# A sign step moved to GpSimd and a subtraction moved to VectorE while the first MLP's weights are unpacked from float64

## The chip, the core and the metric

The kernel runs on one core of one Trainium2 chip. The metric is the device time of one execution in microseconds (us); the time of a kernel is the median of its runs. One execution is also recorded by the hardware profiler, and its rows are what this text reads. TensorE (PE) multiplies matrices, VectorE (DVE), ScalarE (ACT) and GpSimd (POOL) work elementwise on tiles of 128 partitions, and SyncE (SP) issues most transfers. Each engine takes its instructions strictly in the order in which the program put them; engines wait for one another through semaphores.

## What is computed

A delta-rule attention over 4 batches, 8 heads, 768 steps and 48 dimensions gives 3072 rows of 384. Two MLPs follow: one with 2048 hidden units and a PReLU, one with 1536 hidden units and a gated SiLU. Cut to what matters here:

```python
h = x @ w_in                       # 3072x384 by 384x2048
g = np.maximum(h, 0.0) + alpha * np.minimum(h, 0.0)
x = (g @ w_out).astype(np.float32) # 3072x2048 by 2048x384
g = x @ w_gate
val = x @ w_val
out = (silu(g) * val) @ w_out2
```

All weights reach the device as float64. The core has no float64 arithmetic in this kernel: it rebuilds each float32 from the two 32-bit words of a float64 with integer shifts.

## The kernel before

The sequence is cut into 24 chunks of 32 steps. For a window of four chunks the kernel transposes k and q, forms the products k k^T (tile `GL`), inverts a triangular system for all 32 lanes at once (`lanes`: VectorE takes ten columns of it, GpSimd the others, in alternating multiply and subtract steps named `tmp`/`X` and `tmg`/`X`), and then updates the state chunk by chunk (`do_KS`, `do_QS`, `do_U`, `do_S`, `do_Y`, `do_XT`). The result of two chunks is one block of 256 columns for the first MLP. A step of that MLP is `H1` (9 matmuls, then ScalarE and VectorE make the PReLU tile `pn`), `H1_parts` (ScalarE rounds it to the high part, GpSimd subtracts to get the low part, tile `gh`) and, two steps later, `O1` (9 matmuls). Matmul operands are split into a rounded high half and a low half, and three products are added.

The weights of the first MLP are 16 pairs (one slice of `w_in` and one of `w_out`, 384 elements each per partition). `all_w1` (L869) turns a pair from float64 into the two halves. For pair p:

- ScalarE scales the high words in place (`Cut.act`, L592).
- VectorE does three steps in `Cut.dve`: the sign bit into the one scratch tile `we` (z = 0, L597), the high word shifted and joined with that sign (z = 1, L599), the low word shifted and joined (z = 2, L603). Each works on 768 elements per partition.
- ScalarE copies the result, rounded, into the high half of the weight tile (L887).
- The low half is float32 minus high half (`lo`, L875): two operations of 384 elements, both on GpSimd.

The weight tile of pair p lies in the buffer that held the float64 words of pair p-1 (pool `ws`, 17 buffers), so the copy of pair p waits until the low half of pair p-1 has been made. `all_w1` is a generator. `prelude` takes 16 of its 49 steps by hand (`go(conv, ...)`); a list of due times (`at(...)`) spreads the rest over the first eleven MLP steps, three to a step, and so fixes where each instruction stands on its engine. A second user of `Cut`, the weights of the second MLP, works on 384 elements at a time, from due time 24 on.

```python
CONVS = C_A, C_B, C_C, C_D = (1, 3, 3, 1)
for i in range(CONV_N):
    at(-0.5 + i * CONV_END / CONV_N, go, conv)
```

In the names of instructions, `w_110` to `w_125` are the buffers of the float64 words of pairs 0 to 15.

Of the kernel before, what the change touches and what calls it, by code (L numbers as in the profile page):

```python
# [14 lines left out]
ALU = mybir.AluOpType  # L15
# [9 lines left out]
def kernel(  # L25
# [25 lines left out]
    nc = tc.nc  # L51
# [16 lines left out]
    W1_DVE = 16  # L68
# [508 lines left out]
    we = wstg.tile([128, 768], I32, name="we")  # L577
    wf_t = [we[:, 384:768].bitcast(F32), wstg.tile([128, 384], F32, name="wf")]

    class Cut:  # L580
# [13 lines left out]
        def dve(self, z):  # L594
            t, f = self.hi.bitcast(I32), self.f.bitcast(I32)
            if z == 0:
                nc.vector.tensor_scalar(we[:, 0 : self.n], t, -0x80000000, None, op0=ALU.bitwise_and)  # L597
            elif z == 1:
                nc.vector.scalar_tensor_tensor(  # L599
                    out=t, in0=t, scalar=3, in1=we[:, 0 : self.n], op0=ALU.logical_shift_left, op1=ALU.bitwise_or  # L600
                )
            else:
                nc.vector.scalar_tensor_tensor(  # L603
                    out=f, in0=self.lo, scalar=29, in1=t, op0=ALU.logical_shift_right, op1=ALU.bitwise_or
                )
# [18 lines left out]
    def load_w1(*slices, eng=nc.sync):  # L624
        for i in slices:
            load_wide(*w1_src(i), w1_64[i // 2][:, i % 2], eng)
# [242 lines left out]
    def all_w1():  # L869

        cuts = []

        def lo(p, z0, z1, eng):
            f = cuts[p].f.rearrange("p (a n) -> p a n", a=2)
            eng.tensor_tensor(w1[p][:, z0:z1, 1], f[:, z0:z1], w1[p][:, z0:z1, 0], ALU.subtract)  # L875

        for p in range(J1 + 1):
            while len(cuts) < min(J1, p + (1 if p == 0 else 2)):
                cuts.append(Cut(w1_64[len(cuts)]))
                cuts[-1].act()  # L880
            for z in range(3):
                if p < J1:
                    cuts[p].dve(z)
                if z == 0 and p > 0:
                    w1.append(ws.tile([128, 2, 2, 384], F32R, name="w", tag="w"))
                    f = cuts[p - 1].f.rearrange("p (a n) -> p a n", a=2)
                    nc.scalar.activation(out=w1[p - 1][:, :, 0], in_=f, func=AF.Copy)  # L887
                    lo(p - 1, 0, 1, nc.gpsimd)
                    if p <= W1_DVE:
                        lo(p - 1, 1, 2, nc.gpsimd)  # L890
                if z > 0 and W1_SP <= p + W1_AHEAD < J1:
                    load_w1(2 * (p + W1_AHEAD) + z - 1, eng=nc.scalar)
                if z == 1 and p > W1_DVE:
                    lo(p - 1, 1, 2, nc.vector)
                if p < J1 or z == 1:
                    yield

    conv = all_w1()

    def go(g, n=1):  # L900
# [251 lines left out]
```

## Time and profile before

| | us |
|---|---|
| runs | 1094.44, 1092.07, 1091.46 |
| median | 1092.07 |
| the profiled execution | 1094.43 |
| its span, first to last instruction | 1092.5 |
| TensorE busy | 1055.2 (97%) |
| VectorE busy | 603.6 (55%) |
| ScalarE busy | 389.9 (36%) |
| GpSimd busy | 359.5 (33%) |

The profiled execution is 2.36 us longer than the median of the runs. Busy shares are means over stages that differ: the unpacking of the 16 pairs lies between 10 and 116 us of the span, where GpSimd and VectorE are far busier than on average. A busy time holds whatever an engine spends inside an instruction, also when the instruction is held up by another engine. [...]

### The profile page before, as it was taken

How to read it: one execution, taken by the hardware profiler on the slowest of the kernel's cores; microseconds unless marked ns; L12 is line 12 of the kernel's file. 1: busy time of each engine (PE TensorE's matmuls, PEld its weight loads, DVE VectorE, ACT ScalarE, POOL GpSimd, SP SyncE). 2: the span in 40 equal slices, each digit the busy share in tenths (PEclk: the TensorE clock that was granted, in tenths of full speed). 3: DMA queues.
4: the chain of work that ended last, by engine and by line, in shares of the span. 5: the costliest groups of instructions: out<-in, count | busy, mean ns of one | idle time of the engine just before them, and what ended most of it. 6: DMA issues, size and time to landing. Idle time of an engine off the chain costs nothing.

```text
span 1092.5 us, 35673 instructions
## 1 busy us (share of the span) xinstructions
PE 1055.2 (97%) x15649; PEld 969.6 (89%) x15649; DVE 603.6 (55%) x1204; ACT 389.9 (36%) x841; POOL 359.5 (33%) x531
## 2 busy tenths in 40 slices
PE   6689899999999999999999999999999999999998
PEld 5588788999999999999999998888888888888887
DVE  5778865975895697489453453433333333333332
ACT  3556343343434334433444653222222222222211
POOL 3478852832563383366333541101001001010000
PEclk9669999999999999999999999999999999999999
DMA  9663042353344236330441541010010010100001
GB/s 196 184 192 105 10 103 53 62 122 95 70 69 134 66 62 139 90 82 11 118 130 56 159 135 54 1 58 1 1 58 1 18 42 1 58 1 1 29 1 29
DMA packets 165979, 76.34 MB, mean 70 GB/s; under 512 B 129824, under 2 KB 160576, under 8 KB 165824
## 3 DMA queue, kind: packets, MB, share of 16 engines
q1 hardware_dynamic: 160256, 66.28, 24.5%
q10 hardware_dynamic: 5184, 7.37, 2.2%
q8 instruction: 122, 2.00, 0.8%
q0 software_dynamic: 384, 0.41, 0.2%
q14 instruction: 33, 0.27, 0.1%
HBM read 57.52 MB, written 16.52 MB: 68 GB/s over the span
## 4 chain that ended last, share of the span: by engine, by line
PE 89%; POOL 4%; issue 2%; DVE 2%; DMA 1%; ACT 1%; SPq 0%; ACTq 0%; POOLq 0%; DVEq 0%
PE gv L772 27%; PE o L713 18%; PE h L682 18%; PE o L802 14%; PE pst L527 2%; PE pg L207 2%; PE pu L506 2%; PE py L548 2%; PE pk L462 2%; PE py L462 1%; POOL w L875 1%; DMA nat<-in_k_dram 1%; POOL gh L702 1%; POOL X L331 1%; POOL tmg L323 1%
## 5 line engine op out<-in xcount | busy, mean ns | idle before, releaser
L772 PE MATMUL gv<-x2s,w 128*128 128x512 f32 x1296 | 307.6, 391 | 0.0
L772 PEld LDWEIGHTS gv<-x2s,w 128*128 128x128 f32 x1296 | 242.5, 188 | 47.8
L713 PE MATMUL o<-gh,w 128*128 128x256 f32 x1728 | 246.2, 288 | 3.9 <-POOL gh L702 3.9
L682 PE MATMUL h<-xh,w 128*128 128x256 f32 x1152 | 241.2, 286 | 3.0 <-DVE pn L693 1.6
L702 POOL TENSOR_TENSOR gh<-pn,gh 128x256 fp32r<-128x256 f32 x192 | 155.3, 809 | 248.5 <-ACT gh L701 217.3
L713 PEld LDWEIGHTS o<-gh,w 128*128 128x128 f32 x1728 | 217.3, 189 | 11.5 <-POOL gh L702 5.1
L682 PEld LDWEIGHTS h<-xh,w 128*128 128x128 f32 x1152 | 192.2, 191 | 5.8 <-DVE pn L693 2.6
L693 DVE SCALAR_TENSOR_TENSOR pn<-pn,slope,h 128x256 f32<-128x256 f32 x192 | 91.3, 476 | 135.9 <-ACT pn L692 135.9
L682 PE MATMUL h<-xl,w 128*128 128x256 f32 x576 | 163.2, 283 | 0.1
L802 PE MATMUL o<-w,us 128*128 128x384 f32 x864 | 162.5, 337 | 0.0
L802 PEld LDWEIGHTS o<-w,us 128*128 128x128 f32 x864 | 151.9, 188 | 7.1 <-DVE os L815 1.4
L692 ACT ACTIVATE pn<-h,slope 128x256 f32<-128x256 f32 x192 | 90.4, 471 | 137.7 <-PE h L682 134.5
L784 DVE TENSOR_TENSOR sg<-sg,gv 128x512 f32<-128x512 f32 x72 | 49.5, 687 | 151.8 <-ACT sg L782 151.7
L701 ACT ACTIVATE gh<-pn 128x256 fp32r<-128x256 f32 x192 | 80.0, 417 | 145.0 <-DVE pn L693 143.2
L682 PEld LDWEIGHTS h<-xl,w 128*128 128x128 f32 x576 | 109.8, 191 | 0.6 <-DVE xl L574 0.6
L757 POOL TENSOR_TENSOR x2s<-x2r,x2s 128x512 fp32r<-128x512 f32 x15 | 19.3, 1320 | 266.6 <-ACT x2s L755 266.6
L789 ACT ACTIVATE us<-u 128x512 fp32r<-128x512 f32 x72 | 45.5, 632 | 171.2 <-DVE u L785 171.2
L782 ACT ACTIVATE sg<-gv 128x512 f32<-128x512 f32 x72 | 43.0, 597 | 159.3 <-PE gv L772 159.3
L790 DVE TENSOR_TENSOR us<-u,us 128x512 fp32r<-128x512 f32 x72 | 49.9, 693 | 54.8 <-ACT us L789 54.8
L785 DVE TENSOR_TENSOR u<-sg,gv 128x512 f32<-128x512 f32 x72 | 49.5, 688 | 49.3 <-PE gv L772 48.8
L331 DVE TENSOR_TENSOR X<-X,tmp 128x31 f32<-128x31 f32 (+29 forms) x155 | 65.0, 419 | 4.8
L323 DVE TENSOR_TENSOR tmp<-L,X 128x31 f32<-128x31 f32 (+29 forms) x155 | 59.5, 384 | 1.8
(120 smaller groups left out, 975.9 us busy)
## 6 DMA issues: line engine op xcount, KB each, us to landing
w<-in_moe_w_out_dram SPq DMA_DIRECT2D x19, 384.0 KB
wf<-w2d SPq DMA_DIRECT2D x36, 192.0 KB
k<-in_k_dram SPq DMA_DIRECT2D x96, 48.0 KB
x2d<-xs SPq DMA_DIRECT2D x12, 384.0 KB
w<-in_moe_w_gate_dram SPq DMA_DIRECT2D x12, 384.0 KB
w<-in_moe_w_val_dram SPq DMA_DIRECT2D x12, 384.0 KB
x2r<-x2d SPq DMA_DIRECT2D x24, 192.0 KB
v<-in_v_dram SPq DMA_DIRECT2D x88, 48.0 KB
```

The source lines that it names most:

```text
L323: eng.tensor_tensor(w, t.L[:, i + 1:C, i:i + 1].to_broadcast([128, n, m]), t.X[:, i:i + 1, c0:c0 + m].to_broadcast([128, n, m]), ALU.mult,)
L331: eng.tensor_tensor(Xv, Xv, w, ALU.subtract)
L682: nc.tensor.matmul(ps[:, 0:N1], w[:, a, kk * 128:kk * 128 + 128], x[b][:, kk, :], start=(i == 0), stop=(i == 3 * NK - 1),)
L692: nc.scalar.activation(out=g, in_=hv, func=AF.Relu, scale=slope[:, 0, j:j + 1])
L693: nc.vector.scalar_tensor_tensor(out=g, in0=g, scalar=slope[:, 1, j:j + 1], in1=hv, op0=ALU.mult, op1=ALU.add)
L701: nc.scalar.activation(out=gh[:, 0], in_=g, func=AF.Copy)
L702: nc.gpsimd.tensor_tensor(gh[:, 1], g, gh[:, 0], ALU.subtract)
L713: nc.tensor.matmul(o[:, dm // 2, (dm % 2) * N1:(dm % 2) * N1 + N1], w[:, a, dm * 128:dm * 128 + 128], g[:, b], start=(j == 0 and i == 0 an ...
L772: nc.tensor.matmul(p[:, 0:N2], w2[j, z][:, a, kk * 128:kk * 128 + 128], x[:, b, kk], start=(i == 0), stop=(i == 3 * NK - 1),)
L784: nc.vector.tensor_tensor(sg, sg, ps[0], ALU.mult)
L790: nc.vector.tensor_tensor(us[:, 1], u, us[:, 0], ALU.subtract)
L802: nc.tensor.matmul(o2_t[n][t][:, 0:DM], us[:, a, t * 128:t * 128 + 128], w[:, b, :], start=(j == 0 and i == 0), stop=(j == J2 - 1 and i == 2),
```

## The change

For the 768-element pairs, step z = 0 is issued on GpSimd: `is_lt 0.0` gives 1 or 0, the product with -2147483648.0 is written as an int32, which is the sign bit alone. The two low-half subtractions of 384 elements on GpSimd become one of 768 elements on VectorE, and it is issued one generator step later, between z = 1 and z = 2 of the next pair. The 384-element cuts of the second MLP keep the sign on VectorE.

```diff
         def dve(self, z):
             t, f = self.hi.bitcast(I32), self.f.bitcast(I32)
             if z == 0:
-                nc.vector.tensor_scalar(we[:, 0 : self.n], t, -0x80000000, None, op0=ALU.bitwise_and)
+                if self.n > 384:
+                    nc.gpsimd.tensor_scalar(
+                        we[:, 0 : self.n], self.hi, 0.0, -2147483648.0, op0=ALU.is_lt, op1=ALU.mult
+                    )
+                else:
+                    nc.vector.tensor_scalar(we[:, 0 : self.n], t, -0x80000000, None, op0=ALU.bitwise_and)
...
                     nc.scalar.activation(out=w1[p - 1][:, :, 0], in_=f, func=AF.Copy)
-                    lo(p - 1, 0, 1, nc.gpsimd)
-                    if p <= W1_DVE:
-                        lo(p - 1, 1, 2, nc.gpsimd)
                 if z > 0 and W1_SP <= p + W1_AHEAD < J1:
                     load_w1(2 * (p + W1_AHEAD) + z - 1, eng=nc.scalar)
-                if z == 1 and p > W1_DVE:
-                    lo(p - 1, 1, 2, nc.vector)
+                if z == 1 and p > 0:
+                    lo(p - 1, 0, 2, nc.vector)
```

VectorE, around the second pair (`w_111`), at 35 to 40 us of the trace: `TT` is the inverse that the first `do_U` multiplies with, `pi` a product it is corrected by. Before:

```order
L273 STREAM_TRANSPOSE TT<-X 128x16x32
L597 TENSOR_SCALAR we<-w_111 128x768
L599 SCALAR_TENSOR_TENSOR w_111<-w_111,we 128x768
L603 SCALAR_TENSOR_TENSOR w_111<-w_111 128x768
L439 TENSOR_TENSOR TT<-TT,pi 128x16x16
L597 TENSOR_SCALAR we<-w_112 128x768
```

And now:

```order
L273 STREAM_TRANSPOSE TT<-X 128x16x32
L604 SCALAR_TENSOR_TENSOR w_111<-w_111,we 128x768
L880 TENSOR_TENSOR w<-w_110,w 128x2x384
L608 SCALAR_TENSOR_TENSOR w_111<-w_111 128x768
L439 TENSOR_TENSOR TT<-TT,pi 128x16x16
L604 SCALAR_TENSOR_TENSOR w_112<-w_112,we 128x768
```

The sign has left VectorE's row and the subtraction of the pair before stands ahead of the correction of `TT`.

GpSimd, from its last transfers of v to the first unpacked pairs; `X` and `Dm` are cleared, `v` and `mt` are scaled. Before:

```order
L123 DMA v<-in_v_dram 32x8x48 x8
L263 MEMSET X 128x1024
L398 MEMSET Dm 128x32x16
L452 TENSOR_TENSOR v<-v,nn 128x384 x2
L195 TENSOR_TENSOR mt<-mt,mask 128x256 x2
L875 TENSOR_TENSOR w<-w_110,w 128x384 x2
L875 TENSOR_TENSOR w<-w_111,w 128x384 x2
```

And now:

```order
L123 DMA v<-in_v_dram 32x8x48 x8
L598 TENSOR_SCALAR we<-w_110 128x768
L263 MEMSET X 128x1024
L398 MEMSET Dm 128x32x16
L452 TENSOR_TENSOR v<-v,nn 128x384 x2
L195 TENSOR_TENSOR mt<-mt,mask 128x256 x2
L598 TENSOR_SCALAR we<-w_111 128x768
```

One sign stands for two subtractions of a pair, and the first sign comes ahead of the clearing of `X`.

VectorE at the end of the unpacking, at 106 to 116 us, where the second inversion begins with two transposes of `GL` into `L`. Before:

```order
L603 SCALAR_TENSOR_TENSOR w_124<-w_124 128x768
L693 SCALAR_TENSOR_TENSOR pn<-pn,slope,h_1990 128x256
L597 TENSOR_SCALAR we<-w_125 128x768
L599 SCALAR_TENSOR_TENSOR w_125<-w_125,we 128x768
L603 SCALAR_TENSOR_TENSOR w_125<-w_125 128x768
L693 SCALAR_TENSOR_TENSOR pn<-pn,slope,h_2057 128x256
L269 STREAM_TRANSPOSE L<-GL 128x512
```

And now:

```order
L608 SCALAR_TENSOR_TENSOR w_124<-w_124 128x768
L698 SCALAR_TENSOR_TENSOR pn<-pn,slope,h_1976 128x256
L604 SCALAR_TENSOR_TENSOR w_125<-w_125,we 128x768
L880 TENSOR_TENSOR w<-w_124,w 128x2x384
L608 SCALAR_TENSOR_TENSOR w_125<-w_125 128x768
L698 SCALAR_TENSOR_TENSOR pn<-pn,slope,h_2042 128x256
L880 TENSOR_TENSOR w<-w_125,w 128x2x384
L269 STREAM_TRANSPOSE L<-GL 128x512
```

Two subtractions came in, and the last of them stands right ahead of the first transpose.

## Rows read from the trace of the kernel before

**Rows 1.** The page: busy us (share of the span) and instructions of each engine.

```profile
PE 1055.2 (97%) x15649; PEld 969.6 (89%) x15649; DVE 603.6 (55%) x1204; ACT 389.9 (36%) x841; POOL 359.5 (33%) x531
```

**Rows 2.** Stages: length, busy us (instructions) of PE, PEld, DVE, ACT, POOL; clock, DMA.

```profile
34.00:56.00 22.00, 12.02 (x519) 10.38 (x519) 15.60 (x22) 11.90 (x20) 10.09 (x9) 0.59 0.63 158
56.00:84.00 28.00, 25.88 (x725) 24.00 (x725) 21.41 (x26) 15.29 (x30) 19.65 (x16) 0.71 0.66 185
84.00:116.00 32.00, 29.90 (x904) 27.10 (x904) 25.84 (x31) 18.51 (x39) 27.91 (x26) 1.00 0.32 84
116.00:148.00 32.00, 26.47 (x203) 24.21 (x202) 30.09 (x78) 11.21 (x31) 26.19 (x58) 1.00 0.30 57
...
200.00:640.00 440.00, 440.00 (x9148) 424.19 (x9146) 300.02 (x676) 191.47 (x448) 213.89 (x345) 1.00 0.38 92
```

**Rows 3.** Groups: busy us, mean ns, idle before; L875: min/median/max ns instead.

```profile
L875 POOL TENSOR_TENSOR w<-w,w x32: 1009/1225/1793, 36.6 to 113.6; 128x384 fp32r<-128x384 f32 x32
...
L597 DVE TENSOR_SCALAR we<-w 128x768 int32<-128x768 int32 x16 | 11.5, 717 | 3.7 <-ACT w L592 3.7
...
L599 DVE SCALAR_TENSOR_TENSOR w<-w,we 128x768 int32<-128x768 int32 x16 | 18.4, 1153 | 0.5
...
L603 DVE SCALAR_TENSOR_TENSOR w<-w 128x768 int32<-128x768 int32 x16 | 21.4, 1339 | 0.4
...
L693 DVE SCALAR_TENSOR_TENSOR pn<-pn,slope,h 128x256 f32<-128x256 f32 x192 | 91.3, 476 | 135.9 <-ACT pn L692 135.9
...
masks.py:199 POOL TENSOR_SCALAR_AFFINE_SELECT ident<-ident 128x128 f32<-128x128 f32 x1 | 0.3, 293 | 0.1
...
L263 POOL MEMSET X<- 128x1024 f32 x6 | 6.1, 1012 | 1.3 <-DVE L L269 1.3
```

**Rows 4.** Timeline, 35 to 40 us, VectorE and TensorE: start us, us, instruction [idle before].

```profile
35.01 0.56 DVE L597 TENSOR_SCALAR we<-w 128x768 int32<-128x768 int32 x1 [3.32 <-ACT w L592]
...
37.53 0.62 PE L430 MATMUL pi<-tmp,Dm 16*32 16x16 f32 x31 [1.97 <-issue]
...
38.21 0.42 DVE L439 TENSOR_TENSOR TT<-TT,pi 128x256 f32<-128x256 f32 x1 [0.65 <-PE pi L430]
...
38.55 1.27 DVE L597 TENSOR_SCALAR we<-w 128x768 int32<-128x768 int32 x1
```

**Rows 5.** Timeline, 51 to 56 us: what leads to the first MLP matmul.

```profile
51.07 0.78 DVE L995 TENSOR_SCALAR slope<-slope 128x16 f32<-128x16 f32 x1
...
53.36 0.95 DVE L603 SCALAR_TENSOR_TENSOR w<-w 128x768 int32<-128x768 int32 x1
...
53.41 0.90 PE L570 MATMUL px<-ident,ys 128*128 128x128 f32 x3 [0.64 <-ACT ys L557]
...
54.35 0.90 ACT L887 ACTIVATE w<-w 128x768 fp32r<-128x768 f32 x1 [0.17 <-DVE w L603]
...
55.16 0.47 ACT L573 ACTIVATE xh<-px 128x384 fp32r<-128x384 f32 x1
...
55.68 0.58 PE L682 MATMUL h<-xh,w 128*128 128x256 f32 x1 [1.37 <-ACT xh L573]
```

**Rows 6.** Timeline, 105 to 116 us: how the second inversion begins.

```profile
105.55 0.56 DVE L574 TENSOR_TENSOR xl<-px,xh 128x384 fp32r<-128x384 f32 x1 [1.74 <-ACT xh L573]
...
109.02 1.10 PE L207 MATMUL pg<-kqt 48*32 48x64 f32 x64
...
111.66 0.90 ACT L887 ACTIVATE w<-w 128x768 fp32r<-128x768 f32 x1 [2.06 <-POOL w L875]
...
112.47 0.36 ACT L217 ACTIVATE GL<-pg 128x256 f32<-128x256 f32 x1
...
112.87 1.11 DVE L269 STREAM_TRANSPOSE L<-GL 128x512 f32<-128x512 f32 x1 [1.74 <-ACT GL L217]
...
115.22 1.08 DVE L269 STREAM_TRANSPOSE L<-GL 128x512 f32<-128x512 f32 x1
```

**Rows 7.** Timeline, VectorE after the first pair's cut (idle before it in brackets).

```profile
15.47 1.99 DVE L269 STREAM_TRANSPOSE L<-GL 128x512 f32<-128x512 f32 x2 [1.97 <-ACT GL L217]
```

## The prediction, made before the changed kernel was run

> **What bounds the kernel now.** I read the busy shares first [rows 1]: TensorE is busy 97% of the span. Then the stages [rows 2], to see where the missing 3% lies. From 200 to 640 us TensorE has no idle time at all, so nothing that the three elementwise engines do there sets the end. The change works between 10 and 116 us, and what it can win or lose is the time at which TensorE gets through the early stages. There are three of them. From 34 to 56 us TensorE is busy 12.0 of 22 us, on a mean clock of 0.59: it waits for single results, and also sits idle about 2 us at a time with nothing in the profile to release it (the "issue" in [rows 4]). From 56 to 116 us it is busy 55.8 of 60 us: the bound is TensorE itself, half on the half clock until 84 us (mean 0.71) and at full clock after. From 116 to 148 us the second inversion runs on VectorE (30.1 of 32) and GpSimd (26.2 of 32), and TensorE is idle 5.5 us behind it. So the change counts in two places: the chain up to the first MLP matmul at 55.68 [rows 5], and the start of the second inversion, its two transposes at 112.87 and 115.22 [rows 6]. In between, GpSimd's 87% share from 84 to 116 looks like a bound, but TensorE is busy 29.9 of 32 us there, so relief of GpSimd is worth at most about 2 us in that stage.
>
> **What goes and what comes.** GpSimd loses 32 subtractions with a median of 1.225 us, 2.45 us a pair; the quickest of them took 1.009 us [rows 3]. It gains 16 signs on 768 elements. No row shows a tensor-with-scalar comparison on GpSimd with an int32 result, so I bound it. From below: clearing 1024 elements, which reads nothing, takes 1.012 us, so 768 take 0.76. From above: an operation with two inputs takes 1.009 us for 384 elements, so 2.0 for 768. In between stands the one row with one input, the select over 128 elements in 0.293 us: six times that is 1.76, but a fixed part is then counted six times over. I take 1.2 us, nearest to the select less its fixed part, and keep 0.76 to 2.0. Per pair GpSimd then has 1.2 us in place of 2.45.
>
> VectorE loses 16 signs (mean 0.717, unhindered 0.56) and gains 16 subtractions of 768 with two inputs. The nearest rows are the two-input shifts of the same size: 0.95 unhindered [rows 5], 1.15 and 1.34 in the mean [rows 3]. So a pair costs VectorE 0.24 to 0.62 us more. From 84 to 116 us there are about six pairs: 1.5 to 3.7 us on top of 25.8, which stays under 32. This is covered by the idle time of VectorE and by the two MLP steps that lie between an `H1` and its `O1`; without that cover it would be paid in full.
>
> **The chain to 56 us.** The first pair, at 11 us, is covered: VectorE has finished it at 13.50 and then idles 1.97 us until 15.47 [rows 7]. A sign may take 0.56 + 1.97 = 2.5 us before it is seen.
>
> The second pair is not. VectorE's sign began at 35.01, as soon as ScalarE had scaled the pair [rows 4], and GpSimd, idle then, can begin at that time too. VectorE must now wait for it, and then does z = 1, the subtraction of the first pair and z = 2, 3 x 0.96 plus 0.04 between each, before the correction of `TT`. That ends at 35.01 + 1.2 + 3.0 = 39.2, where `TT` began at 38.21: 1.0 us later (0.55 with a sign of 0.76 us, 1.8 with 2.0). TensorE's first `do_U` waits for just that and moves by the same. What is queued behind the waiting VectorE is this correction; who waits for it is TensorE.
>
> On top there is interference. The sign of the third pair becomes ready when z = 1 of the second ends, so it runs against the subtraction or z = 2. In the trace VectorE's sign at 38.55 took 1.27 us instead of 0.56 while GpSimd subtracted [rows 4], 0.71 more. I take half of that, 0.35, with ends 0 and 0.7.
> [...]
>
> The rest of the chain to 56 us shifts along. The subtractions add about 1 us a pair to VectorE and wait for ScalarE's copies, which before they did not. In return GpSimd no longer works against the slope operations, of which one took 0.78 us for 16 elements [rows 5]. I put these at zero together, within -0.8 and +1. The lower end: TensorE's `px` transposes end at 54.3, so `xh` could start there and not at 55.16 behind the copy (54.35) that waits for VectorE. So the first MLP matmul moves from 55.68 by 1.0 + 0.35 = +1.35 us, between -0.25 and +3.5. From there TensorE is the bound and carries the shift on.
>
> **The second inversion.** In the trace ScalarE's last copy waited 2.06 us for GpSimd's subtraction and held `GL` until 112.47 [rows 6]. That wait goes. What is late next: the copy now needs z = 2 and the subtraction on VectorE. I add up from `xl` at 105.55, which hangs on TensorE, with 0.96 a step and 0.47 for `pn` [rows 3]: z = 2 to 107.1, `pn` to 107.55, z = 1 to 108.5, subtraction to 109.5, z = 2 to 110.5. The copy takes 0.90, to 111.4; the last subtraction waits for it and ends at 112.4, and the first transpose follows, 0.45 us sooner than 112.87. The second transpose stands behind a `pn` and the state update and comes 0.4 sooner than 115.22. The inversion carries this through to 148 us, since TensorE is idle 5.5 us behind it. The ends are -2.3 (`GL` right after its product, at 110.1) and 0.
>
> **Sum.** +1.35 - 0.4 = +0.95 us. The profiled execution would go from 1094.43 to 1095.4; on the median of the runs, 2.36 us lower, it is 1092.07 + 0.95 = 1093.0. With the ends of the two places, -2.5 to +3.5, it is 1089.5 to 1095.6.
>
> **Rivals.**
> (a) *The sign is slow on GpSimd*, and the kernel is slower. Place: VectorE at z = 1 of the first and second pair. Price: 0.55 us at 35 us for a sign of 0.76, then one for one, and again one for one at 11 us beyond 2.5 us. With 4 us: 3.8 + 0.35 + 1.5 - 0.4 = +5.2, so 1097.3. It decides, beyond 0.3% (3.3 us), from a sign of about 3.1 us on. For it: no row shows the instruction. Against it: GpSimd's quickest subtraction, with two inputs, took 2.6 ns an element [rows 3].
> (b) *The first use of the instruction on GpSimd is slow.* At 11 us VectorE would wait. In the trace no first use on GpSimd shows a pause of that kind: the first select took 0.293 us with 0.1 idle before it [rows 3]. Of a pause, 2.5 - 1.2 = 1.3 us are covered by VectorE's idle time and the rest is paid in full; beyond 0.3% it decides from 3.7 us on (1.3 + 3.3 - 0.95), where the time is 1095.4, and each us more adds one.
> [...]
> (c) *The relief wins.* The delay of `do_U` disappears in an "issue" gap after it, `xh` starts at 54.3, and `GL` at 110.1: -0.8 - 2.3 = -3.1, 1089.0. For it: the 2.06 us wait and the gaps. Against: the subtraction that now stands ahead of both.
> (d) *VectorE becomes the bound from 56 to 116 us*, by waiting for ScalarE's copies. 0.6 us a pair over ten pairs, less 4.2 us that TensorE has idle there, is about +2 on top of the forecast: 1095.
> (e) *Nothing comes through*: the shifts cancel, 1092.
>
> **How the numbers follow.** The forecast has 0.50, (e) 0.18, (c) 0.12, (a) 0.09, (d) 0.08, (b) 0.03. 0.3%, about what a measurement of this kernel can tell from no change, is 3.3 us: 1088.8 to 1095.4. Half of (c) lies under it: 0.06, and 0.01 for a luckier clock. Over it lie (a), (b), a third of (d) and the upper tail of the forecast: 0.09 + 0.03 + 0.03 + 0.03 = 0.18. The remaining 0.75 is no change. The range runs from the lower end of the sum, 1089.5, to 1096.5, past (d) but short of (a) and (b).
>
> **What would show it.** The GpSimd group `we<-w` 128x768 with a mean of 0.8 to 2.0 us; the correction of `TT` near 39.5 instead of 38.21; the first `h` matmul near 57 instead of 55.68; the second transpose `L<-GL` 0.9 us later than 115.22, that is 0.4 sooner counted from that matmul; GpSimd's busy time from 84 to 116 down by some 8 us with TensorE's idle time there about as it was. The prediction is wrong if the sign takes over 3 us, if TensorE waits for `pn` or `gh` between 56 and 116 us, or if the half-clock stretches get longer or shorter by more than the shift.

## The result, and the profile of the changed kernel

The changed kernel takes 1098.76 us (median; 1097.35 to 1100.50). The kernel before, run beside it, takes 1093.12 (1091.46 to 1094.65). The ratio is 1.0053 with a 95% interval from 1.0039 to 1.0067: slower by 5.6 us, beyond the forecast range of 1089.5 to 1096.5, on the side that had a chance of 0.18.

The two profiled executions, 1097.35 and 1094.43 us, differ by 2.9 us only. The first is the quickest of its kernel's runs, the second among the slower ones of its own. So rows show where time goes, and its size is taken from the medians.

The page of the changed kernel: busy us, share and instructions of each engine, to be held against [rows 1].

```profile
PE 1053.3 (96%) x15649; PEld 968.0 (88%) x15649; DVE 607.6 (55%) x1204; ACT 389.6 (36%) x841; POOL 371.3 (34%) x515
```

GpSimd has 16 instructions fewer and is busy 11.8 us longer. The stages of the changed kernel: length, busy us (instructions) of PE, PEld, DVE, ACT, POOL; TensorE's granted clock (1.00 is full, 0.50 half), DMA share, GB/s.

```profile
34.00:56.00 22.00, 11.61 (x518) 10.02 (x518) 13.79 (x20) 10.73 (x18) 15.26 (x5) 0.58 0.56 145
56.00:84.00 28.00, 24.88 (x725) 22.92 (x726) 23.59 (x26) 16.54 (x32) 23.66 (x11) 0.75 0.69 191
84.00:116.00 32.00, 28.04 (x835) 25.60 (x835) 25.87 (x28) 16.68 (x34) 26.80 (x14) 1.00 0.30 87
116.00:148.00 32.00, 25.96 (x245) 23.54 (x244) 30.14 (x74) 10.84 (x32) 24.10 (x51) 0.95 0.17 38
...
200.00:640.00 440.00, 440.00 (x9154) 424.36 (x9153) 300.76 (x682) 190.10 (x447) 213.99 (x347) 1.00 0.38 93
```

Against [rows 2], the late part is as it was: TensorE has no idle time from 200 to 640 us. From 56 to 116 us it is busy 24.88 + 28.04 = 52.92 of 60 us where it was 55.78, so 2.9 us more idle time stand in the stage that was taken to be TensorE's own; 1.1 of them lie ahead of the first MLP matmul, which now begins at 57.07, and the rest behind it, nearly all of it in one stop of 2.04 us (below): the idle times that nothing releases add up to 4.1 us here and to 4.2 before. From 84 to 116 us GpSimd went from 27.91 to 26.80, not down by eight.

The groups that the change made: the sign in two views (busy us, mean ns, and idle time before it; then min/median/max ns), z = 1 that waits for it, and the subtraction.

```profile
L598 POOL TENSOR_SCALAR we<-w 128x768 int32<-128x768 f32 x16 | 53.2, 3323 | 12.4 <-ACT w L592 3.5 <-DVE w L604 3.0 <-DMA v<-in_v_dram 2.7
...
L598 POOL TENSOR_SCALAR we<-w x16: 2808/3468/3552, 11.6 to 108.4; 128x768 int32<-128x768 f32 x16
...
L604 DVE SCALAR_TENSOR_TENSOR w<-w,we 128x768 int32<-128x768 int32 x16 | 17.5, 1097 | 19.5 <-POOL we L598 17.4 <-DMA nat<-in_k_dram 2.1
...
L880 DVE TENSOR_TENSOR w<-w,w 128x768 fp32r<-128x768 f32 x16 | 19.6, 1222 | 3.5 <-ACT w L892 3.5
```

A sign takes 2.81 us at its quickest and 3.47 in the median. VectorE stood idle 17.4 us for it. Three things tell how the delay travels. The first is the second pair, 35 to 57 us (timeline: start us, us, instruction, idle time before it and what ended it):

```profile
34.95 2.82 POOL L598 TENSOR_SCALAR we<-w 128x768 int32<-128x768 f32 x1 [2.06 <-issue]
...
37.80 0.96 DVE L604 SCALAR_TENSOR_TENSOR w<-w,we 128x768 int32<-128x768 int32 x1 [5.37 <-POOL we L598]
...
38.91 3.39 POOL L598 TENSOR_SCALAR we<-w 128x768 int32<-128x768 f32 x1 [1.14 <-DVE w L604]
...
39.54 1.61 DVE L608 SCALAR_TENSOR_TENSOR w<-w 128x768 int32<-128x768 int32 x1
...
41.08 0.41 DVE L439 TENSOR_TENSOR TT<-TT,pi 128x256 f32<-128x256 f32 x1
...
44.90 0.86 PE L475 MATMUL pk<-U,mx 32*32 32x48 f32 x32 [0.35 <-issue]
...
57.07 0.58 PE L687 MATMUL h<-xh,w 128*128 128x256 f32 x1 [2.19 <-ACT xh L573]
```

The correction of `TT` is 2.87 us later than in [rows 4], the first MLP matmul 1.39 later than in [rows 5]. The second is pair 11, in the middle of the first MLP (same columns):

```profile
83.49 1.11 POOL L707 TENSOR_TENSOR gh<-pn,gh 128x256 fp32r<-128x256 f32 x1 [0.47 <-ACT gh L706]
...
84.56 1.45 POOL L195 TENSOR_TENSOR mt<-mt,mask 128x256 f32<-128x256 f32 x1
...
85.98 3.53 POOL L598 TENSOR_SCALAR we<-w 128x768 int32<-128x768 f32 x1
...
89.55 1.48 DVE L604 SCALAR_TENSOR_TENSOR w<-w,we 128x768 int32<-128x768 int32 x1 [2.13 <-DMA nat<-in_k_dram]
...
91.82 1.63 DVE L608 SCALAR_TENSOR_TENSOR w<-w 128x768 int32<-128x768 int32 x1
...
93.54 0.90 ACT L892 ACTIVATE w<-w 128x768 fp32r<-128x768 f32 x1 [2.47 <-DVE w L608]
...
94.33 0.38 ACT L221 ACTIVATE mt<-pg 128x256 f32<-128x256 f32 x1
...
94.76 1.10 PE L207 MATMUL pg<-kqt 48*32 48x64 f32 x64 [2.04 <-ACT mt L221]
```

Read downwards, this is one queue after another. GpSimd makes `gh` and `mt` first, then the sign, which ends at 89.51. VectorE begins z = 1 at 89.55: the wait is put down to a transfer of k, but it ends with the sign. ScalarE's copy waits 2.47 us for VectorE. Behind the copy, in ScalarE's order, stands the small read of `pg`, which frees the bank that the next `pg` products need, and TensorE stops for 2.04 us. The third is the last two pairs, ahead of the second inversion:

```profile
106.85 1.49 DVE L604 SCALAR_TENSOR_TENSOR w<-w,we 128x768 int32<-128x768 int32 x1 [1.89 <-POOL we L598]
...
108.42 3.47 POOL L598 TENSOR_SCALAR we<-w 128x768 int32<-128x768 f32 x1 [0.91 <-DVE w L604]
...
111.93 0.96 DVE L604 SCALAR_TENSOR_TENSOR w<-w,we 128x768 int32<-128x768 int32 x1 [0.79 <-POOL we L598]
...
115.27 0.90 ACT L892 ACTIVATE w<-w 128x768 fp32r<-128x768 f32 x1 [2.46 <-DVE w L608]
...
119.41 1.15 DVE L269 STREAM_TRANSPOSE L<-GL 128x512 f32<-128x512 f32 x1
...
123.48 0.38 PE L687 MATMUL h<-xh,w 128*128 128x256 f32 x1 [1.53 <-DVE pn L698]
```

The scratch tile `we` is one, so the last sign could begin only when z = 1 of pair 14 had read the one before (0.91 us). The copy waits 2.46 us where [rows 6] had 2.06, now for VectorE. The second transpose is at 119.41, not 115.22. How much of this is made here is seen from the first matmul of the twelfth MLP step, behind which TensorE's clock is full; before, changed kernel, and the kernel of the first experiment below, which has the low half on VectorE and the sign there too:

```profile
111.21 0.28 PE L682 MATMUL h<-xh,w 128*128 128x256 f32 x1
```

```profile
112.80 0.28 PE L687 MATMUL h<-xh,w 128*128 128x256 f32 x1
```

```profile
109.73 0.28 PE L682 MATMUL h<-xh,w 128*128 128x256 f32 x1
```

From there to the second transpose it is 4.01 us before, 6.61 in the changed kernel and 4.14 with the low half alone (113.87, below).

### The profile page after: what moved, and what is told of

Its sections match the earlier page's. It is cut to its first block, busy times and chain, and to the rows that moved or that the text cites. A ratio compares the mean times of both kernels' runs of the same rounds, so it can differ in the third digit from the quotient of the medians.

```text
span 1095.6 us, 35658 instructions
## 1 busy us (share of the span) xinstructions
PE 1053.3 (96%) x15649; PEld 968.0 (88%) x15649; DVE 607.6 (55%) x1204; ACT 389.6 (36%) x841; POOL 371.3 (34%) x515
## 4 chain that ended last, share of the span: by engine, by line
PE 90%; DVE 3%; POOL 3%; issue 2%; DMA 1%; ACT 1%; SPq 0%; ACTq 0%; DVEq 0%; POOLq 0%
PE gv L777 27%; PE o L718 18%; PE h L687 18%; PE o L807 14%; PE pst L527 2%; PE pu L506 2%; PE pg L207 2%; PE pk L462 2%; PE py L548 2%; PE py L462 1%; DMA nat<-in_q_dram 1%; POOL X L331 1%; PE px L570 1%; POOL gh L707 1%; POOL tmg L323 1%
```

## The experiments

Diffs are against the changed kernel; a ratio is that of medians to the kernel before, run beside it. `k` is the number of the pair (`cuts[-1].k = len(cuts) - 1`).

### The two halves apart

The low half on VectorE, with the sign left there:

```diff
             if z == 0:
-                if self.n > 384:
-                    nc.gpsimd.tensor_scalar(
-                        we[:, 0 : self.n], self.hi, 0.0, -2147483648.0, op0=ALU.is_lt, op1=ALU.mult
-                    )
-                else:
-                    nc.vector.tensor_scalar(we[:, 0 : self.n], t, -0x80000000, None, op0=ALU.bitwise_and)
+                nc.vector.tensor_scalar(we[:, 0 : self.n], t, -0x80000000, None, op0=ALU.bitwise_and)
```

> The sign is back on VectorE; the low half stays one VectorE subtraction of 768 elements, issued where the change put it. Theory A (the sign of 2.8 to 3.5 us on GpSimd, for which VectorE waits 17.4 us in all, is what costs): VectorE's wait before z = 1 is gone, VectorE has 0.56 us more work a pair, GpSimd is nearly free; within 2 us of the kernel before, 1092 to 1095. Theory B (the subtraction that stands on VectorE ahead of TT's correction, of the second inversion's transposes, and waits for ScalarE's copy is what costs): as the changed kernel, 1097.5 or more.

Measured: 0.9984 [0.9975, 0.9992], 1092.87 us: faster than both kernels. Rows of this run, the groups of z = 1 and of the subtraction, then the first MLP matmul and the second transpose:

```profile
L599 DVE SCALAR_TENSOR_TENSOR w<-w,we 128x768 int32<-128x768 int32 x16 | 15.6, 976 | 0.4
...
L875 DVE TENSOR_TENSOR w<-w,w 128x768 fp32r<-128x768 f32 x16 | 17.4, 1088 | 4.3 <-ACT w L887 4.3
...
56.40 0.58 PE L682 MATMUL h<-xh,w 128*128 128x256 f32 x1 [1.43 <-ACT xh L573]
...
113.87 1.13 DVE L269 STREAM_TRANSPOSE L<-GL 128x512 f32<-128x512 f32 x1
```

VectorE's z = 1 fell from 1153 to 976 ns and waits 0.4 us in all. The subtraction's 1.09 us are hidden: the time is no longer than before. The second transpose comes 1.35 us sooner than before although the first matmul comes 0.72 later; but these 2.07 us all lie between the fourth and the fifth MLP step, and largely in TensorE's clock (see below), so the rows of one execution each do not show what gives the 1.6 thousandths. The whole loss, 6.9 thousandths of the kernel before or about 7.5 us, is the sign's.

The sign on GpSimd, with the low half left there as two operations:

```diff
+                    lo(p - 1, 0, 1, nc.gpsimd)
+                    if p <= W1_DVE:
+                        lo(p - 1, 1, 2, nc.gpsimd)
...
-                if z == 1 and p > 0:
-                    lo(p - 1, 0, 2, nc.vector)
+                if z == 1 and p > W1_DVE:
+                    lo(p - 1, 1, 2, nc.vector)
```

> The sign on GpSimd as changed; the low half is two GpSimd subtractions again, as before the change. Theory A: GpSimd then has 3.3 + 2.7 + 1.1 = 7 us a pair where pairs came every 5.2 us, and z = 1 waits for it; some 1.8 us for each of the last ten pairs, at least 10 us above the kernel before: 1103 to 1120. Theory B: near the kernel before, 1092 to 1096.

Measured: 1.0239 [1.0225, 1.0253], 1119.52 us. At its quickest the sign takes as long as in the changed kernel; on a GpSimd that also subtracts, it stands in a longer queue, and VectorE waits 47.7 us for it instead of 17.4. The line of the sign in this run, and who waited for it (us, times):

```profile
L598 POOL TENSOR_SCALAR we<-w x16: 2802/2830/3546, 11.6 to 131.1; 128x768 int32<-128x768 f32 x16
...
  DVE w L604: 47.7, 15
```

### Why the sign takes 2.8 us

Neither a comparison nor an integer result:

```diff
-                        we[:, 0 : self.n], self.hi, 0.0, -2147483648.0, op0=ALU.is_lt, op1=ALU.mult
+                        we[:, 0 : self.n].bitcast(F32), self.hi, 0.0, 0.0, op0=ALU.min, op1=ALU.mult
```

> As changed, but the sign is made as a signed float zero: the smaller of the value and 0.0, times 0.0, written as float32 bits; two operations on 768 elements as in the change, no comparison and no int32 result. Theory A1 (the comparison or the int32 result makes the instruction slow): the sign takes 0.8 to 2.0 us and the time is 1092 to 1095.5. Theory A2 (any tensor-with-scalar operation on GpSimd over these words, 8 bytes apart, takes that long): 2.8 us and more, and the time is that of the changed kernel, 1098 to 1100.

Measured: 1.0053 [1.0040, 1.0065], the ratio of the changed kernel to the digit. Half the elements on GpSimd, half on VectorE:

```diff
-                        we[:, 0 : self.n], self.hi, 0.0, -2147483648.0, op0=ALU.is_lt, op1=ALU.mult
+                        we[:, 0:384], self.hi[:, 0:384], 0.0, -2147483648.0, op0=ALU.is_lt, op1=ALU.mult
                     )
+                    nc.vector.tensor_scalar(we[:, 384:768], t[:, 384:768], -0x80000000, None, op0=ALU.bitwise_and)
```

> As changed, but GpSimd signs 384 of the 768 elements and VectorE the other 384 (0.36 us). Theory A: a sign of about 1.45 us in place of 2.8; most of VectorE's 17.4 us of waiting goes, and the time falls by 2 to 5 us from the changed kernel, to 1094 to 1097. Theory B: nothing is won, VectorE has 0.36 us more a pair; 1098 to 1101.

Measured: 0.9987 [0.9977, 0.9996], 1092.53 us: more is won than either expectation had. One operation in place of two:

```diff
-                        we[:, 0 : self.n], self.hi, 0.0, -2147483648.0, op0=ALU.is_lt, op1=ALU.mult
+                        we[:, 0 : self.n].bitcast(F32), self.hi, 0.0, None, op0=ALU.mult
```

> As changed, but the sign is one operation in place of two: the value times 0.0, written as float32 bits, a signed zero. If the second arithmetic step of the instruction is what makes it slow: 1.2 to 2.0 us, and the time falls to 1092 to 1096. If the instruction's way of reading, or its scalar operands, set it: 2.8 us again, 1098 to 1100.

Measured: 0.9997 [0.9987, 1.0007], 1094.34 us; VectorE waits 13.4 us for it. The time is that of the first expectation, the sign's duration (2.16 us at its quickest, 2.79 in the median) that of neither. An input whose elements lie next to each other (the high words are 8 bytes apart), which leaves the sign out of the weights:

```diff
-                        we[:, 0 : self.n], self.hi, 0.0, -2147483648.0, op0=ALU.is_lt, op1=ALU.mult
+                        we.rearrange("p (a b) -> p a b", a=6), ident.unsqueeze(1).to_broadcast([128, 6, 128]),
+                        0.0, -2147483648.0, op0=ALU.is_lt, op1=ALU.mult
```

> As changed, but the sign instruction reads a constant 128x128 tile six times, elements next to one another, in place of the high words, which lie 8 bytes apart (the sign bits of the weights are left out, and the instruction no longer waits for ScalarE). Only the duration counts. If the distance of 8 bytes is what makes it slow: under 2 us; if not: 2.8 us unhindered, as with the words.

Measured in one run: 1099.04 us. The sign's line in these four, in their order (min/median/max ns):

```profile
L598 POOL TENSOR_SCALAR we<-w x16: 2807/3402/3547, 11.6 to 110.8; 128x768 f32<-128x768 f32 x16
```

```profile
L598 POOL TENSOR_SCALAR we<-w x16: 1521/2097/2239, 11.5 to 103.2; 128x384 int32<-128x384 f32 x16
```

```profile
L598 POOL TENSOR_SCALAR we<-w x16: 2164/2787/2954, 11.7 to 104.2; 128x768 f32<-128x768 f32 x16
```

```profile
L598 POOL TENSOR_SCALAR we<-ident x16: 2775/3417/3485, 11.7 to 108.7; 128x768 int32<-128x768 f32 x16
```

Comparison, integer result and the 8 bytes are not what costs: the minimum stays at 2.8 us. Elements and operations are: 384 elements fewer save 1.29 us, so an element takes (2.807 - 1.521) / 384 = 3.35 ns with two operations and 0.24 us are left over for the instruction; one operation less saves 0.64 us. What makes an element this slow on GpSimd stays open.

### Where a slow sign costs

The sign on GpSimd for some of the pairs only. First the five pairs that are cut ahead of the first MLP matmul, and the eleven others:

```diff
-                if self.n > 384:
+                if self.n > 384 and self.k < 5:
```

> As changed, but only pairs 0 to 4 (cut before 56 us) have their sign on GpSimd; pairs 5 to 15 have it on VectorE. Theory: the sign costs in two places, the chain to the first MLP matmul, and the chain of the last pairs before the second inversion. Early part alone: the first matmul is 0.7 us later than with all signs on VectorE (57.07 against 56.40), so 1092.9 + 0.7, 1093 to 1095. Rival (the early delay sets everything, as the prediction had it): 1097 to 1099, the time of the changed kernel.

Measured: 0.9996 [0.9985, 1.0006]. With `self.k >= 5`:

> As changed, but only pairs 5 to 15 have their sign on GpSimd; pairs 0 to 4 have it on VectorE. Theory of the two places: the late part carries the greater share, 5.9 - 0.7 us over the 1092.9 of the kernel with all signs on VectorE, 1096 to 1099, and the second transpose of the second inversion comes 4 to 6 us later than in that kernel (113.87). Rival (the early delay sets everything): 1092 to 1094.

Measured: 1.0039 [1.0025, 1.0052]. The place that the prediction priced, pairs 0 and 1, is among those that give no measurable loss against the kernel before; nearly all of it comes with the later pairs. These split again, into the last two, `self.k >= 14`:

> As changed, but only the last two pairs, 14 and 15, have their sign on GpSimd. With all signs on VectorE the time is 0.9984 of the kernel before, with pairs 5 to 15 on GpSimd 1.0039. Theory: the last two signs stand between TensorE's work and the start of the second inversion, which is GpSimd's and VectorE's own, so what they lose there is not made up: the second transpose comes 1.5 to 2.5 us later than with all signs on VectorE, counted from the same matmul, and the time is 1.000 to 1.001 of before (1094 to 1095.5). Rival (the signs of the middle pairs make the whole loss): 0.998 to 0.999.

Measured: 0.9995 [0.9985, 1.0004], between the two expectations; and the middle, `5 <= self.k < 14`:

> As changed, but only pairs 5 to 13 have their sign on GpSimd. Theory: between 56 and 100 us TensorE stops for ScalarE at one product (2.04 us with all signs, 3.02 us with pairs 5 to 15 on GpSimd), because ScalarE's copy stands behind VectorE, and VectorE behind the sign; that part gives 2 to 3.5 us over the kernel with all signs on VectorE, 1.000 to 1.002 of before (1094.5 to 1096.5). Rival (the last two pairs make the whole loss): 0.998 to 0.999.

Measured: 1.0018 [1.0006, 1.0031]. The middle without pair 11, `5 <= self.k < 14 and self.k != 11`:

> As the kernel with the signs of pairs 5 to 13 on GpSimd (1.0018 of before), but pair 11 has its sign on VectorE. Pair 11's sign stands on GpSimd behind two other operations, VectorE waits 2.36 us for it, ScalarE's copy 3.75 us for VectorE, and TensorE 3.00 us for ScalarE's next operation but one. If this one chain is the middle pairs' loss: TensorE's stop at that product goes, and the time is 0.998 to 1.000 of before. If the loss is spread over the nine pairs (longer waits and interference at each): a ninth of it goes, 1.001 to 1.002.

Measured: 1.0004 [0.9992, 1.0016], between the two expectations. Every pair but 11, `self.k != 11`:

> As the changed kernel (1.0053 of before), but pair 11 alone has its sign on VectorE. One chain: 2 to 3 us less than the changed kernel, 1.002 to 1.0035. Spread: 1.0045 to 1.0055.

Measured: 1.0023 [1.0011, 1.0034], inside the range for one chain: one sign less on GpSimd, and 3.0 thousandths of the 5.3 are gone, with intervals that do not meet. The profiled executions of the two are equally long (1097.42 and 1097.35 us), so their rows show the place and not the size. The group of matmuls behind the read of `pg`, at about 92 to 95 us, in five kernels: low half only, middle, middle without 11, all without 11 (the changed kernel's is the 2.04 us stop above).

```profile
92.38 0.76 PE L207 MATMUL pg<-kqt 48*32 48x64 f32 x40 [0.33 <-issue]
```

```profile
95.05 1.23 PE L207 MATMUL pg<-kqt 48*32 48x64 f32 x64 [3.00 <-ACT mt L221]
```

```profile
93.48 1.43 PE L207 MATMUL pg<-kqt 48*32 48x64 f32 x64 [1.57 <-ACT mt L221]
```

```profile
94.32 0.76 PE L207 MATMUL pg<-kqt 48*32 48x64 f32 x40 [1.09 <-issue]
```

The stop for `mt` is there when pair 11 has its sign on GpSimd, and gone when it has not and the pairs ahead of the middle are on GpSimd too. In the middle without pair 11 a shorter one is left, so other pairs reach TensorE the same way. The kernel before stands still at this place too, for 1.21 us and without a releaser:

```profile
94.12 0.76 PE L207 MATMUL pg<-kqt 48*32 48x64 f32 x40 [1.21 <-issue]
```

The ratio by kernel, with readings of one timeline each: first MLP matmul, second transpose, the time between them, the last part of it from the twelfth step's first matmul on, and TensorE's mean granted clock from 56 to 84 us.

| sign on GpSimd for pairs | ratio | first MLP matmul | second transpose | between them | from the twelfth step | clock |
|---|---|---|---|---|---|---|
| kernel before | 1 | 55.68 | 115.22 | 59.54 | 4.01 | 0.71 |
| none (low half only) | 0.9984 | 56.40 | 113.87 | 57.47 | 4.14 | 0.76 |
| 0 to 4 | 0.9996 | 58.24 | 116.62 | 58.38 | 4.10 | 0.72 |
| 14, 15 | 0.9995 | 57.11 | 115.96 | 58.85 | 6.04 | 0.75 |
| 5 to 13 without 11 | 1.0004 | 56.78 | 116.23 | 59.45 | 4.54 | 0.91 |
| 5 to 13 | 1.0018 | 56.51 | 117.89 | 61.38 | 4.13 | 0.90 |
| all without 11 | 1.0023 | 56.63 | 118.75 | 62.12 | 7.07 | 0.79 |
| 5 to 15 | 1.0039 | 55.04 | 118.31 | 63.27 | 6.31 | 0.93 |
| all (changed kernel) | 1.0053 | 57.07 | 119.41 | 62.34 | 6.61 | 0.75 |

The time between the two readings holds the clock, which differs from execution to execution. The last part does not: the clock is full in all nine there, and the signs of pairs 14 and 15 put the second transpose 1.9 to 2.9 us later than with the low half alone wherever they are on GpSimd. Behind the stop for `mt` the clock fell to half for about 3 us in three of these executions (5 to 13 without 11, 5 to 13, 5 to 15: 0.50 from 96 to 97 us) and stayed full in the changed kernel; what the stop costs by itself and what by the clock behind it, no run separates.

Against the low half alone, the early pairs add 1.2 thousandths, the middle 3.4, the last two 1.1. Only the middle's interval stands clear of the low half's. The three add up to 5.7 of the 6.9, which fits within the intervals. That the difference of these medians holds none of the clock is not shown.

### Other engines for it

The sign by ScalarE, whose product with 0.0 seems to come out without the sign, so that this kernel's weights lack theirs (its output is off by 2603.66, relative to the reference, as is that of the kernel above that leaves the sign out):

```diff
-                    nc.gpsimd.tensor_scalar(
-                        we[:, 0 : self.n], self.hi, 0.0, -2147483648.0, op0=ALU.is_lt, op1=ALU.mult
+                    nc.scalar.activation(
+                        out=we[:, 0 : self.n].bitcast(F32), in_=self.hi, func=AF.Copy, scale=0.0
```

> The low half as changed; the sign is made by ScalarE, as the value times 0.0, a signed zero (0.9 us, as its other operations on 768 elements). VectorE has 0.57 us less a pair than with the sign on itself, ScalarE 0.9 us more; ScalarE was busy 19.3 of 32 us from 84 to 116. If VectorE's work per pair still limits: faster than with the sign on VectorE, 0.996 to 0.998 of before. If the wait of VectorE for a ScalarE that itself stands behind TensorE costs more than that: 0.999 to 1.003.

Measured: 1.0008 [0.9998, 1.0019]. The operation takes 0.90 us there, yet VectorE waits for it as long as for GpSimd's, since it is queued behind ScalarE's other work:

```profile
L604 DVE SCALAR_TENSOR_TENSOR w<-w,we 128x768 int32<-128x768 int32 x16 | 15.3, 959 | 18.5 <-ACT we L598 17.4 <-DMA nat<-in_k_dram 1.1
```

The sign on VectorE, and the low half shared, 384 elements on GpSimd and 384 on VectorE (the edit of the sign, as in the first experiment, is left out here):

```diff
+                if z == 0 and p > 0:
+                    lo(p - 1, 0, 1, nc.gpsimd)
                 if z == 1 and p > 0:
-                    lo(p - 1, 0, 2, nc.vector)
+                    lo(p - 1, 1, 2, nc.vector)
```

> All signs on VectorE; of the low half GpSimd makes 384 elements and VectorE the other 384. If it was relief of GpSimd that made the kernel with the whole low half on VectorE faster than before, half of it gives part of the gain: 0.998 to 0.9995 of before; if VectorE's extra work cost something there, sharing gives more: below 0.998.

Measured: 0.9998 [0.9988, 1.0007], not better than all of it on VectorE. It falls into neither range, so what gives the gain of the low half alone stays open. The best version found is the change without its sign, at 0.9984; half a sign on GpSimd, 0.9987, can't be told from it.

## Why the prediction was wrong

**The sign's duration** was the term that was mis-sized: "I take 1.2 us, nearest to the select less its fixed part, and keep 0.76 to 2.0." It measured 2.81 unhindered and 3.47 in the median. The upper bound took the two-input subtraction, 1.009 us for 384 elements [rows 3], to be dearer than any operation with one input. It is not: 2.6 ns an element there, 3.35 here. That row was a neighbour, not a bound. The experiment that halved the elements brought the sign to 1.52 us at its quickest (2.10 in the median), and the loss went with it (0.9987).

**"From there TensorE is the bound and carries the shift on"** is the step that failed with it, and the place of rival (a). The rival had the right cause, a slow sign, deciding from 3.1 us on, with a chance of 0.09. It put the price at the first two pairs. The runs put it elsewhere: the early pairs alone give 0.9996, the middle and the end 1.0039. A share of 93% busy was read as a bound with slack for everyone else. But TensorE's work there is bound to the elementwise engines by banks and tiles that are freed in order, and a sign that is 2.9 us slower than VectorE's 0.56 lengthens a chain through three engines' queues until it exceeds that slack. The prediction named as its own refutation that TensorE "waits for `pn` or `gh`" from 56 to 116 us. It waited for neither there, but 2.04 us for the read of `pg` into `mt`, which stood on no list. Its two other signs of being wrong did show: the sign takes over 3 us in the median, and the half-clock stretches changed by more than the shift (below).

In the offsets of the MLP steps the stop is mixed with TensorE's clock. The changed kernel is 1.4 us behind at the first matmul of the fourth step (72.91 for 71.50) and 1.4 us ahead at that of the fifth (78.12 for 79.52). What lies between, first before, then in the changed kernel (the last line of each is the stage row from 76 to 79 us, with the clock third from its end):

```profile
75.32 0.62 PE L462 MATMUL pk<-St,kqt 48*32 48x48 f32 x27 [1.97 <-issue]
...
77.23 2.10 PE L713 MATMUL o<-gh,w 128*128 128x256 f32 x9
...
76.00:79.00 3.00, 3.00 (x72) 2.88 (x63) 2.85 (x3) 0.00 (x0) 3.00 (x3) 0.51 0.90 294
```

```profile
75.45 0.49 PE L462 MATMUL pk<-St,kqt 48*32 48x48 f32 x27 [0.70 <-issue]
...
76.59 1.34 PE L718 MATMUL o<-gh,w 128*128 128x256 f32 x9
...
76.00:79.00 3.00, 3.00 (x81) 2.94 (x70) 2.68 (x5) 1.98 (x5) 2.80 (x2) 1.00 0.95 235
```

So 1.3 of the 2.8 us are an idle time that shrank, and the rest is the clock: behind its longer idle time the kernel before ran at half clock, the changed kernel at full. That is luck of the two executions or a gain of the change; one trace of the kernel before does not tell. At the thirteenth step the changed kernel is 1.6 us behind (117.09 for 115.50). Of these 3.0 us, 1.9 are lost between the fifth and the sixth step, mostly in idle times that nothing releases, and 1.1 between the seventh and the ninth: 0.5 with the stop for `mt`, which stands in place of the 1.21 us of the kernel before, and 0.6 behind it. Against the low half alone, whose clock is full from 76 us on as well, 1.9 us are lost from the seventh to the tenth.

**The chain to 56 us** came out near 57 as forecast, 57.07, but by luck: errors of both signs cancel. The correction of `TT` moved by 2.87 us instead of 1.0 + interference. 1.6 us of the difference are the sign (2.82 for 1.2) and 0.3 the interference: z = 2 took 0.66 us longer where 0.35 was put. Then 2.3 came back: the first `pk` products, whose idle time of 1.99 us without a releaser shrank to 0.35, were only 1.21 us late at 44.90 (43.69 before), and the transposes `px`, behind another such gap, 0.57 at 53.98 (53.41). The last 0.8 came from an order of instructions: `xh` stands behind ScalarE's copy, and the copy waits for z = 2 on VectorE, 1.4 us later than in [rows 5].

```profile
53.98 0.90 PE L570 MATMUL px<-ident,ys 128*128 128x128 f32 x3 [0.90 <-ACT ys L557]
...
55.75 0.89 ACT L892 ACTIVATE w<-w 128x768 fp32r<-128x768 f32 x1 [1.03 <-DVE w L608]
...
56.54 0.48 ACT L573 ACTIVATE xh<-px 128x384 fp32r<-128x384 f32 x1
```

The prediction allowed such gaps to swallow a delay only in rival (c), and put the queue behind the copy at zero. The first pair was not covered, though it was said to be: its sign began at 11.58, behind GpSimd's own transfers, and VectorE's first two transposes came at 16.29 instead of 15.47 [rows 7]; but of these 0.8 us nothing is left at 34.95, where the second pair's sign begins (35.01 before).

**The second inversion** was to come 0.4 us sooner, counted from the first MLP matmul; it came 62.34 - 59.54 = 2.80 later. The wait for GpSimd's subtraction did go, as said. What is late next was named too, z = 2 and the copy behind it; with the signs of pairs 14 and 15 at 3.5 us, both moved. From the twelfth MLP step's first matmul on, where the clock is the same, the changed kernel takes 2.6 us more than before (6.61 for 4.01). With the sign on VectorE it is 4.14: no relief shows even without the slow sign, neither the 0.4 us of the forecast nor the 2.3 of its lower end, since the copy then waits for z = 2 on VectorE in place of GpSimd's subtraction.

**GpSimd's relief** of 8 us from 84 to 116 was 1.1. Five signs in that stretch take 17.54 us of its 26.80; with 1.2 us each they would have taken 6.

**Right:** the subtraction's cost on VectorE and its cover. It took 1.222 us against 0.717 for the sign it replaced, 0.5 us more per pair (0.24 to 0.62 forecast), and the run with that half alone shows it hidden. Rival (d), VectorE held up by ScalarE's copies, did not happen: the subtraction waited 3.5 us for them in all. Rival (b) did not happen either: the first sign, at 11.58 us, took 2.81 us like the quickest of the others; it began right behind GpSimd's transfers, without idle time. No row or run shows a pause of that kind, so none gives (b) a time beyond the 1095.4 that the prediction worked out for one of 3.7 us.

**Sum.** At the second transpose the delay is 1.39 + 2.80 = 4.2 us, where 0.95 was forecast. The rows can't be followed to the end: the profiled executions differ by 2.9 us, the medians by 5.6, so at that point the profile no longer decides. Open is also how the middle's loss divides among its pairs: without pair 11 about half of it is gone (1.0018 to 1.0004), with overlapping intervals; only beside all other signs is pair 11's part clear of the noise.

## What to carry to other kernels

Bound the price of an operation that no row shows by rows of the same kind, or leave the upper end open and say at which price the answer turns; fewer inputs did not make an element cheaper here (3.35 ns with one, 2.6 with two). TensorE, busy 93% of a stretch before, still stopped for 2.04 us in the changed kernel, where the work that frees its banks stood in order behind a slow instruction two engines away: follow the moved result through each engine's queue to the next bank or tile that is freed, not only to its first reader. Before rows of two executions are held against each other, compare TensorE's granted clock in the same stretches: here one half-clock stretch in the trace before looked like a gain of the change. When a change has two halves, price and run them apart: here one half gains 1.6 thousandths and the other loses 6.9.

## What the runs showed of the hardware

- A tensor-with-scalar operation on GpSimd took 2.81 us at its quickest for 128x768 with two operations (3.35 ns an element and 0.24 us) and 2.16 with one; VectorE's sign took 0.56 for the same elements. With a float32 output it took 2.81 too, and with input elements next to each other, in place of 8 bytes apart, 2.78.
- GpSimd and VectorE slowed each other in some places and not in others, and did not shut each other out. VectorE's z = 2 at 39.54 (1.61 us, 0.95 alone [rows 5]) began and ended while the sign at 38.91 ran (3.39 us, 2.82 alone): both came out some 0.6 us longer, and z = 2 ended at 41.15, with 1.15 us of the sign, which had started first, still to come. The next pair's z = 2, at 46.12, ran wholly beside the sign at 44.51, and they took 0.95 and 2.82 us.
- GpSimd's product with 0.0 keeps the sign: the kernel that takes the sign from this product alone (2.16 us) gives the reference's output. ScalarE's copy with a scale of 0.0 appears to lose it: that kernel's output has a relative error of 2603.66, the same as the output of the one that leaves the sign out.
- TensorE's granted clock, in slices of 1 us from 34 to 132 us, reads 1.00 or 0.50 before and in the changed kernel; a value between stands in nine of the 196 slices, where it goes from one to the other.
- TensorE's clock fell from full to half behind idle times of TensorE of 1.97 us (75.3, before) and 3.00 us (95.05, signs of pairs 5 to 13), and also of 1.57 us (93.48, 5 to 13 without 11), and stayed full behind one of 2.04 us (94.76, changed kernel), so the length of an idle time alone did not decide it. Nine `o` matmuls took 2.10 us in the half-clock stretch and 1.34 at full clock.
- A wait that the profile puts down to a transfer (2.13 us at 89.55) ended with a GpSimd instruction, at 89.51. Where the releaser named can't be the one, the queue of every engine that the instruction depends on has to be read.
